# Nystrom attention and a multiplicative FFN on one core: another written order of the steps, and a later opening of the up products' buffer

## The chip, the core and the metric

The kernel runs on one core of a Trainium2 chip. The metric is the device time of one execution in microseconds (us); smaller is better. All durations are in us unless ns is written. TensorE (PE) does the matmuls, VectorE (DVE) and ScalarE (ACT) read its results out of PSUM, GpSimd (POOL) adds up landmarks and issues loads, SyncE (SP) issues loads and stores.

## The reference

Eight batches of eight heads, 576 tokens, head size 64. Attention goes through 32 landmarks per head, each the mean of 18 neighbouring rows, with a pseudo-inverse by six Newton steps; the FFN multiplies two linear maps of the result and applies two more.

```python
q_lm = q.reshape(B, H, m, S // m, D).mean(axis=3)      # m = 32; k_lm likewise
A, Bm, C = sm(q, k_lm), sm(q_lm, k_lm), sm(q_lm, k)    # softmax of scaled scores
Z = Bm.transpose(0, 1, 3, 2) / (norm_1(Bm) * norm_inf(Bm) + 1e-06)   # norms over all of Bm
for _ in range(6):
    Z = 2 * Z - Z @ Bm @ Z
x = (A @ Z @ C @ v)          # then heads joined: 4608 tokens x 512
out = (((x @ w1) * (x @ w2)) @ w3) @ w_out             # 512 -> 1024 -> 1024 -> 512
```

## The kernel before

The kernel is a set of Python generators, one per piece of work. Each `yield` ends a step. A text, `ORDER`, lists the steps of all pieces, 1,065 words: each occurrence of a word runs that piece's next step. The five engines run by themselves, each takes its own instructions in the order in which they were written, and semaphores make an instruction wait for its inputs and for its buffer. So the text alone sets the order on every engine and every queue.

A word's last number is the batch, the landmark chain (`CHAINS`: batches 0; 1, 2; 3, 4; 5, 6, 7), the weight part or the group of rows. Where a digit stands ahead of the point, it is a part of the piece.

The weights' product comes first, W = w3 @ w_out in eight row blocks:

- `K`: one warm-up matmul (L593), after seven that stand ahead of the order. `KC`: constants in six steps; the fifth is an addition and six copies on VectorE (L615, L617).
- `S.c`: w_out's row block c is split into two fp16 halves, on ScalarE, then VectorE. `T0.j`, `T1.j`: four transposes of w3's block j (L523), then a copy on ScalarE and a split on VectorE (L529); T0.0 does this in two halves. `F.j`: eight steps of three matmuls each (L537), then a copy out.
- `L`, `LO`: loads of w3 and w_out parts on SyncE. `P`, `FV`: a small copy on GpSimd, which holds the load of the next step on SyncE back. `GT.n`: a small copy on GpSimd that reads a weight part (GT.0: part 4 of w_out), so that the loads behind it in GpSimd's queue wait till the part is there. `LW.1`, `LW.0`: the up weights w2 and w1, two loads each, on GpSimd.

For each batch b:

- `LQ`, `LK`: q and k in halves, loads on GpSimd; `LV`: v on SyncE. `TQ`, `TK`: turned by VectorE (L165). `SQ`, `SK`: landmark sums (L194 to L205) in two steps, on VectorE for batch 0, else on GpSimd. `E.b`: the landmarks' exchange, for batches 0 and 1 by two matmuls and a copy, later by copies on ScalarE (L223).
- `A`, `B`, `C`: the three score matmuls (L326, L241, L269) with exponentials on ScalarE; C is then turned on VectorE. `N`, `R`: norms and squares; `I0` to `I5`: the Newton steps (L389). `V`: landmark values in three groups of matmuls (L347, L353). `M0`, `M1`: row sums of A by a matmul with ones (L366), two passes of ScalarE, one of VectorE. `Z`: Z times the values (L415).
- `G0` to `G3`: Z C v times the up weights (L438), copied out by ScalarE (G0, G2) or VectorE (G1, G3). `U0` to `U7`: the up matmuls, four for w1 (L453), a copy on ScalarE (L458), four for w2 (L453), the product on VectorE (L460) into the buffer `ab`, one for two batches, of which there are two.
- `W.n`: the down matmuls for 128 tokens in two halves of four (L495), a copy on ScalarE (L501), two stores on SyncE. W.35 is done in two column halves (L476).

PSUM has three large buffers (`big()`), used by T, E, C (two), A (two), V, M, I, G, each half of U and some W, and one each of `small()` and `acc()`. A step that opens a large one waits until the last reader of the buffer's former contents is done. The tile shapes in the profile tell two kinds of TensorE steps apart: K, F, T, E, N, M, Z, U and W use the full array (128\*128), while A, B, C, I, R (32\*32), G and V (64\*32) use tiles of it.

The pool `pab` with the buffers `ab` takes the memory of `pf`, which holds the weights' product's inputs. In the kernel before, `pf` is closed and `ab` opened when a U word first occurs:

```python
    for word in ORDER.split():
        if word not in live:
            if word[0] == "U":
                if not pab:
                    pf_scope.__exit__(None, None, None)
                    pab.append(ctx.enter_context(tc.tile_pool(name="pab", bufs=2)))
                open_ab(int(word[3:]))
```

Of the kernel before, what the change touches and what calls it, by code (L numbers as in the profile page):

```python
# [42 lines left out]
F.5 T1.6 V.0 I4.0 V.0 F.5 T0.7 LV1.3 I4.0 F.6 F.6 E.1 F.6 TQ0.2 I4.0 I5.0 E.1 F.6 F.6 I5.0 T1.7 Z.0
SK0.2 Z.0 F.6 T0.7 A.1 Z.0 A.1 T1.7 F.6 F.6 TQ1.3 LQ0.3 A.1 SK1.2 LV3.1 LW.1 LK0.4 G2.0 G0.0 F.6 F.7
T1.7 F.7 G0.0 M0.0 C.1 TQ0.3 LK1.3 SQ0.2 M1.0 G2.0 F.7 C.1 F.7 F.7 C.1 F.7 F.7 C.1 C.1 LQ0.4 G3.0
SQ1.2 G1.0 E.2 E.2 LV1.1 F.7 U0.0 G3.0 B.1 U0.0 G1.0 V.1 U0.0 U4.0 B.1 V.1 TK0.3 U4.0 B.1 V.1 U0.0
U1.0 U4.0 N.1 TK1.3 V.1 LQ1.4 U5.0 U1.0 U4.0 N.1 U5.0 U5.0 U1.0 U2.0 U5.0 U2.0 SK0.3 U1.0 R.1 U3.0
R.1 R.1 U2.0 U3.0 LQ0.5 I0.1 U3.0 LK0.5 SK1.3 U2.0 I0.1 I0.1 U7.0 U3.0 I1.1 F.7 U7.0 I1.1 TK0.4 I1.1
U6.0 W.0 LV0.2 M1.1 U6.0 U6.0 M1.1 U6.0 U7.0 I2.1 U7.0 M0.1 M1.1 M0.1 W.0 I2.1 I2.1 A.2 LV2.2 LK1.5
LK1.4 W.0 I3.1 I3.1 W.1 A.2 I3.1 I4.1 M1.1 M0.1 I4.1 A.2 W.1 I4.1 W.1 I5.1 TQ0.4 I5.1 C.2 Z.1 C.2  # L50
Z.1 I5.1 M0.1 W.2 C.2 Z.1 G0.1 TQ1.4 TK1.4 G1.1 W.2 G0.1 W.0 G1.1 U0.1 U2.1 LV1.2 C.2 U0.1 U0.1 U1.1
W.2 U1.1 SQ0.3 SQ1.3 C.2 W.3 G2.1 SQ0.4 LV3.2 U0.1 U2.1 G3.1 G2.1 V.2 V.2 V.2 U2.1 G3.1 V.2 U1.1
U2.1 SQ1.4 U1.1 U3.1 LQ1.5 U3.1 W.3 TQ0.5 U3.1 SK0.4 U4.1 E.3 SK1.4 LV1.4 U3.1 Z.2 W.3 M0.2 U4.1 Z.2
U7.1 M0.2 U7.1 M0.2 LV2.4 LK1.6 U4.1 E.3 E.4 TK0.5 U5.1 U4.1 U7.1 LV3.3 W.2 LQ0.6 U6.1 U7.1 LV2.3
U5.1 LV3.4 U6.1 Z.2 W.4 E.4 TQ1.5 M1.2 M1.2 U5.1 U6.1 TK1.5 U5.1 B.3 G2.2 M1.2 U6.1 G1.2 G2.2 G0.2
G1.2 W.4 M0.2 G0.2 A.3 M1.2 W.4 G3.2 A.3 A.3 G3.2 LQ1.6 B.3 SK0.5 W.3 W.1 W.5 U3.2 U3.2 C.3 B.3
LQ1.7 C.3 W.5 N.3 LK0.6 W.4 SK1.5 U2.2 LV0.3 LQ0.7 U0.2 C.3 U0.2 N.3 LK1.7 C.3 R.3 U3.2 W.5 U3.2
U0.2 U2.2 U0.2 W.6 SQ0.5 U2.2 U4.2 U2.2 R.3 SQ1.5 U4.2 C.3 W.6 M0.3 M0.3 U1.2 U1.2 W.6 U4.2 U6.2
TQ0.6 V.3 U4.2 U6.2 R.3 V.3 U1.2 U1.2 U6.2 U6.2 W.7 LK0.7 U5.2 I0.3 W.7 U5.2 I0.3 U7.2 I0.3 TQ1.6
I1.3 TK0.6 I1.3 U7.2 W.7 V.3 U7.2 I1.3 W.5 I2.3 W.8 V.3 I2.3 I2.3 TK1.6 W.7 U7.2 I3.3 I3.3 I3.3 W.8  # L60
M1.3 I4.3 I4.3 W.8 LV0.4 U5.2 I4.3 W.9 U5.2 M1.3 I5.3 W.8 M1.3 A.4 M0.3 A.4 W.9 W.9 I5.3 I5.3 M1.3
Z.3 SK0.6 Z.3 A.4 W.6 W.9 C.4 W.10 M0.3 C.4 Z.3 G3.3 W.10 C.4 W.10 G1.3 G3.3 C.4 G0.3 G2.3 W.11 G0.3
U2.3 G1.3 G2.3 U1.3 U2.3 C.4 U2.3 V.4 U1.3 U2.3 SK1.6 E.5 U1.3 U0.3 TQ0.7 V.4 V.4 SQ0.6 LV2.5 U0.3
LV1.5 U1.3 E.5 TQ1.7 M0.4 V.4 U3.3 M0.4 U3.3 M0.4 U3.3 W.11 U0.3 TK0.7 U3.3 U5.3 TK1.7 W.11 U4.3
SQ1.6 Z.4 U0.3 U5.3 LV1.6 U4.3 U5.3 LV0.5 U5.3 A.5 E.6 A.5 Z.4 A.5 W.12 M1.4 M1.4 LV3.6 U7.3 Z.4 E.6
U4.3 M0.4 U4.3 U7.3 M1.4 U7.3 W.12 W.11 U6.3 U7.3 M1.4 G0.4 W.12 U6.3 LV0.6 G1.4 SQ0.7 G0.4 G1.4
G2.4 W.13 SQ1.7 W.10 G2.4 C.5 C.5 SK0.7 LV3.5 U6.3 C.5 U6.3 SK1.7 U1.4 W.13 U1.4 U0.4 E.7 LV2.6 C.5
C.5 V.5 E.7 V.5 G3.4 B.5 U0.4 U0.4 W.13 W.14 B.5 U0.4 G3.4 W.14 U3.4 W.14 B.5 U2.4 V.5 U3.4 U1.4 N.5
U1.4 U2.4 W.13 W.15 W.15 N.5 U2.4 R.5 V.5 W.15 U2.4 R.5 A.6 W.16 U4.4 A.6 A.6 U4.4 M0.5 R.5 I0.5
W.14 M0.5 I0.5 I0.5 W.12 U4.4 U4.4 U5.4 I1.5 U5.4 I1.5 U3.4 I1.5 U3.4 M0.5 U5.4 U6.4 U5.4 I2.5 I2.5  # L70
U7.4 M0.5 U6.4 I2.5 U7.4 U6.4 U6.4 I3.5 W.16 I3.5 M1.5 I3.5 I4.5 W.16 M1.5 W.17 C.6 I4.5 I4.5 I5.5
M1.5 I5.5 W.17 I5.5 C.6 Z.5 M1.5 W.17 Z.5 U7.4 Z.5 W.18 W.17 I5.5 G0.5 C.6 G1.5 W.16 U7.4 G0.5 G2.5
W.18 G1.5 U0.5 U1.5 C.6 G2.5 U0.5 U1.5 U1.5 C.6 U0.5 U2.5 U1.5 V.6 V.6 U0.5 U2.5 G3.5 LV3.7 W.18
U3.5 W.19 U3.5 U3.5 G3.5 U2.5 U3.5 U2.5 W.19 U4.5 W.19 U5.5 U4.5 V.6 M0.6 U5.5 U5.5 W.18 V.6 M1.6
M0.6 LV0.7 Z.6 LV2.7 LV1.7 U5.5 M1.6 U6.5 U4.5 U6.5 W.20 Z.6 M1.6 M0.6 Z.6 G0.6 G1.6 W.19 U4.5 G2.6
W.20 G0.6 M1.6 G3.6 G1.6 G2.6 A.7 W.20 G3.6 M0.6 W.21 W.20 A.7 W.21 U7.5 A.7 U6.5 W.21 U7.5 U0.6
U7.5 U6.5 U0.6 W.22 U7.5 U0.6 W.15 U2.6 U2.6 U0.6 W.22 U1.6 C.7 W.22 W.23 U1.6 C.7 W.22 W.23 M1.7
C.7 W.23 U1.6 U3.6 W.24 W.24 C.7 M1.7 U1.6 U2.6 U5.6 U3.6 U4.6 W.24 W.25 U2.6 W.24 U5.6 W.25 C.7
M1.7 U3.6 U3.6 W.25 V.7 W.23 V.7 U4.6 V.7 W.25 V.7 U4.6 W.26 U4.6 U6.6 U6.6 Z.7 U5.6 M0.7 M1.7 W.26
Z.7 M0.7 U7.6 U6.6 U5.6 W.26 U7.6 U6.6 M0.7 W.27 W.21 Z.7 U7.6 M0.7 G0.7 G1.7 U7.6 G1.7 G0.7 W.27  # L80
U1.7 U1.7 G2.7 W.27 G2.7 G3.7 U1.7 U1.7 W.28 U4.7 U4.7 W.28 W.28 U5.7 U3.7 W.26 G3.7 U5.7 U4.7 W.29
W.28 U4.7 U3.7 U5.7 U3.7 W.29 W.29 W.29 U3.7 U5.7 U0.7 U0.7 U2.7 W.27 U0.7 U7.7 U0.7 U2.7 W.30 U6.7
U7.7 U2.7 U7.7 U2.7 W.30 U6.7 U7.7 U6.7 W.31 W.30 U6.7 W.31 W.32 W.32 W.33 W.33 W.31 W.32 W.30 W.33
W.34 W.31 W.34 W.34 W.35 W.32 W.33 W.35 W.34 W.35 W.35 W.35 W.35
"""


# [1 line left out]
def kernel(  # L89
# [358 lines left out]
    def up(st, j):  # L448
        for w in range(2):
            p = big()  # L450
            for qd in range(2):
                for c in range(2):
                    nc.tensor.matmul(p[:, c, 0:HS], st["g"][:, qd, w, 128 * j:128 * j + 128],  # L453
                                     st["ahat", qd][:, c, :], start=(qd == 0), stop=(qd == 1))
            yield
            if w == 0:
                a_sb = po.tile([128, 2, HS], FP16, name="a_sb", bufs=2)
                nc.scalar.copy(out=a_sb, in_=p[:, :, 0:HS])  # L458
# [246 lines left out]
```

## Time and profile before

| | |
|---|---|
| time, median of 3 runs | 261.96 us (261.48 to 262.25) |
| span of the profiled execution | 260.5 us |
| the profiled execution's own time | told as its span only; 1.5 us lie between it and the median |
| TensorE busy | 249.7 us (96% of the span) |
| VectorE, ScalarE, GpSimd busy | 161.5, 159.2, 119.3 us |
| first warm-up matmul, first transpose | 1.19 us, 4.16 us |
| last matmul starts | 256.1 us |

The span runs from the first to the last instruction of one profiled execution. [...]

### The profile page before, as it was taken

What the parts mean: (1) busy time and instruction counts of PE and PEld (TensorE: products, weight loads), DVE (VectorE), ACT (ScalarE), POOL (GpSimd) and SP (SyncE); (2) the same over time, 40 slices, a digit from 0 to 9 for tenths busy, and PEclk for the clock granted to TensorE, in tenths of its full rate; (3) what the DMA queues carried; (4) which work ended last, traced back from release to release, by engine and by line L of the source; (5) the groups of instructions that cost most, each with busy time, mean ns of one, the idle gap of its engine ahead of it and who ended that gap; (6) DMA issues with size and microseconds to landing.
All of it is one profiled execution on the core that took longest, in us unless ns stands there. A gap on an engine that the chain in (4) does not pass through costs nothing.

```text
span 260.5 us, 10306 instructions
## 1 busy us (share of the span) xinstructions
PE 249.7 (96%) x4480; PEld 147.9 (57%) x4480; DVE 161.5 (62%) x306; ACT 159.2 (61%) x349; POOL 119.3 (46%) x199
## 2 busy tenths in 40 slices
...
DMA packets 23357, 37.37 MB, mean 143 GB/s; under 512 B 2832, under 2 KB 11536, under 8 KB 23312
## 3 DMA queue, kind: packets, MB, share of 16 engines
...
## 4 chain that ended last, share of the span: by engine, by line
PE 82%; DVE 7%; ACT 5%; DMA 2%; issue 2%; SPq 0%; DVEq 0%; ACTq 0%
PE big L453 21%; PE acc L495 20%; PE acc L537 13%; PE big L438 5%; PE big L347 4%; PE big L389 4%; PE big L523 3%; PE small L537 2%; ACT a_sb L458 2%; DVE ab L460 2%; PE big L366 2%; PE big L495 1%; DMA wof<-in_moe_w_out_dram 1%; PE small L415 1%; PE big L326 1%
## 5 line engine op out<-in xcount | busy, mean ns | idle before, releaser
L453 PE MATMUL big<-ahat,gt 128*128 128x288 f16 x512 | 74.3, 286 | 1.3 <-ACT a_sb L458 0.7
L460 DVE TENSOR_TENSOR ab<-a_sb,big 128x576 f16<-128x576 f16 x64 | 47.1, 750 | 35.3 <-PE big L453 33.5
L495 PE MATMUL acc<-w,ab 128*128 128x512 f16 x264 | 66.7, 380 | 0.0
L453 PEld LDWEIGHTS <-gt 128*128 128x128 f16 x512 | 48.5, 98 | 22.0 <-issue 3.0
L458 ACT CAST a_sb<-big 128x576 f16<-128x576 f32 x64 | 40.2, 639 | 33.2 <-PE big L453 18.8
L194 POOL TENSOR_TENSOR tr<-qkT 128x256 f32<-128x256 f16 x56 | 37.3, 697 | 18.2 <-DVE qkT L165 16.3
L537 PE MATMUL acc<-wsp,w3t 128*128 128x512 f16 x168 | 41.6, 384 | 0.0
L495 PEld LDWEIGHTS <-ab 128*128 128x128 f16 x280 | 25.4, 98 | 27.0 <-issue 4.8
L537 PEld LDWEIGHTS <-w3t 128*128 128x128 f16 x192 | 18.4, 100 | 19.8 <-issue 3.1
L501 ACT ACTIVATE o_sb<-acc 128x512 f32<-128x512 f32 x33 | 19.8, 599 | 10.8 <-PE acc L495 9.5
L445 DVE TENSOR_SCALAR gt<-big 128x1024 f16<-128x1024 f32 x16 | 19.4, 1220 | 7.9 <-PE big L438 7.9
L165 DVE STREAM_TRANSPOSE qkT<-qkn 128x576 uint32<-128x576 uint32 x32 | 24.0, 762 | 0.0
L200 POOL TENSOR_TENSOR tr<-tr 128x256 f32<-128x256 f32 x28 | 19.8, 727 | 0.1
L443 ACT ACTIVATE gt<-big 128x1024 f16<-128x1024 f32 x16 | 15.7, 1024 | 3.4 <-PE big L438 3.3
L438 PE MATMUL big<-wup,zt 64*32 64x512 f16 x512 | 17.3, 379 | 0.3 <-ACT en L370 0.2
L347 PE MATMUL big<-vt,ent 64*32 64x64 f32 x1152 | 14.8, 225 | 0.1
L128 POOL DMA_DIRECT2D qkn<-in_k_dram x16 | 11.5, 722 | 6.9 <-DVE qkT L165 6.9
L347 PEld LDWEIGHTS big<-vt,ent 64*32 64x32 f32 x1152 | 12.7, 105 | 3.4 <-issue 2.3
L284 DVE STREAM_TRANSPOSE ent<-en 128x576 f32<-128x576 f32 x16 | 12.0, 762 | 3.3 <-ACT en L280 3.3
L375 DVE TENSOR_TENSOR ahat<-eat,en 128x576 f16<-128x576 f16 x16 | 13.8, 870 | 0.0
L280 ACT ACTIVATE en<-big 128x288 f32<-128x288 f32 x32 | 12.8, 415 | 0.5 <-PE big L269 0.5
L527 ACT ACTIVATE w3t<-big 128x512 f16<-128x512 f32 (+1 forms) x17 | 9.6, 571 | 5.6 <-PE big L523 5.3
...
## 6 DMA issues: line engine op xcount, KB each, us to landing
...
wof<-in_moe_w_out_dram SPq DMA_DIRECT2D x6, 256.0 KB, 7.4
```

The costliest lines, as they stand in the source:

```text
L165: nc.vector.transpose(out=st["qkT"][:, t, prs].rearrange("p c r q e -> p (c r q e)").bitcast(U32), in_=st["qkn"][:, t, prs, :].rearrange(" ...
L194: add(out=tr[:, c], in0=x[:, c, 0:4, :], in1=x[:, c, 4:8, :], op=ALU.add)
L200: add(out=tr[:, c, 0:2, :], in0=tr[:, c, 0:2, :], in1=tr[:, c, 2:4, :], op=ALU.add)
L347: nc.tensor.matmul(psV[32 * o:32 * o + 32, qd, 0:64], ent[sl, pr, r, :], vt[sl, pr, 64 * r:64 * r + 64], start=(r == 0), stop=(r == RT - 1 ...
L438: nc.tensor.matmul(psG[o:o + 32, qd, :], zt[rs, i, h, :], wup[rs, h, w, fs], start=(i == 0), stop=(i == 1), tile_position=(64 * qd, o))
L445: nc.vector.tensor_scalar(out=g[:, :, w, fs], in0=psG, scalar1=1.0 / ZS, scalar2=None, op0=ALU.mult)
L453: nc.tensor.matmul(p[:, c, 0:HS], st["g"][:, qd, w, 128 * j:128 * j + 128], st["ahat", qd][:, c, :], start=(qd == 0), stop=(qd == 1))
L458: nc.scalar.copy(out=a_sb, in_=p[:, :, 0:HS])
L460: nc.vector.tensor_tensor(out=st["ab"][:, j, st["t0"]:st["t0"] + S].rearrange("p (c s) -> p c s", c=2), in0=a_sb, in1=p[:, :, 0:HS], op=AL ...
L495: nc.tensor.matmul(pso[:, :], ab[:, j, t0:t0 + 128], w34[:, j, :], start=(j == 0), stop=(j == 7))
L501: nc.scalar.activation(out=o_sb, in_=pso, func=AXF.Copy, scale=1.0 / (X64 * X64))
L537: nc.tensor.matmul(psW, w3ts[j, c // 4][:, a, c % 4, :], wsp[:, b, c, :], start=(c == 0 and a + b == 0), stop=(c == 7 and a == 1))
```

## The change

The words of `ORDER` are written in another order; none is added or taken away. `open_ab` is called in `up`, just ahead of the product on VectorE, instead of ahead of a U word's first step, and closes `pf` there. The core of the diff follows; of the order, the first lines and those that hold the steps the prediction speaks of.

```diff
 ORDER = """
-T0.0 S.0 S.0 T0.0 T0.0 T0.0 T0.1 S.2 S.2 LQ0.0 T0.1 K LQ1.0 S.1 T0.1 L.2 LO.6 S.3 F.0 K F.1 S.1
-LK0.0 T0.0 KC F.0 LK1.0 T0.0 T1.0 F.0 T1.0 S.3 S.4 K T1.0 S.5 S.4 F.1 K FV.0 F.1 F.0 T1.1 T1.1 K S.6
-F.0 S.5 T1.1 KC LO.7 KC F.1 F.1 T1.2 F.1 TQ1.0 T1.2 GT.0 LK1.1 L.3 T0.2 LK0.1 S.7 F.0 S.6 F.1 TQ0.0
...
-C.0 GT.5 F.3 B.0 F.3 C.0 N.0 T0.5 KC T1.4 TQ1.1 N.0 LW.0 F.3 T1.4 T1.4 SK0.1 C.0 TQ0.1 F.4 LV2.1 F.4
-T0.5 F.4 A.0 T0.5 R.0 R.0 R.0 F.4 F.4 F.4 LQ0.2 A.0 I0.0 I0.0 T0.6 LV0.1 SK1.1 L.7 I0.0 A.0 T0.6 C.0
...
-M0.0 M1.0 C.0 TK1.2 F.5 V.0 V.0 TQ1.2 M1.0 T1.6 I3.0 F.5 F.5 TK0.2 I3.0 F.5 M1.0 I3.0 LK0.3 F.5 T0.7
...
+K GT.0 S.0 K KC K T0.0 T0.1 LQ1.0 K T0.0 T0.1 L.2 S.0 S.1 S.2 LQ0.0 T0.0 T0.1 K S.3 LO.6 F.0 T0.0
+S.1 LK1.0 S.4 T0.0 LK0.0 F.1 LO.7 LK1.1 T1.0 S.2 F.1 F.1 S.5 T1.0 F.0 LQ0.1 T1.1 T0.0 F.0 S.3 L.3
+S.5 T1.0 S.4 S.6 F.1 T0.2 T1.1 F.0 S.7 LK0.1 T0.2 LQ1.1 S.6 T1.1 F.0 T1.2 T1.2 S.7 F.0 F.0 T0.2 T1.2
+KC TQ1.0 F.0 FV.0 P.4 F.1 F.0 T0.3 T1.3 F.2 F.2 F.2 F.2 P.4 F.2 GT.2 T0.3 T1.3 F.2 F.2 L.5 F.2 T0.3
+F.1 F.2 F.1 F.1 TQ0.0 F.3 F.3 SQ0.0 TK1.0 SQ1.0 TK0.0 F.3 F.3 SK0.0 T1.3 SK1.0 F.3 TQ0.1 F.1 FV.0
+E.0 T0.4 LQ0.2 E.0 LK0.2 KC TK1.1 F.3 TK0.1 C.0 T0.4 KC B.0 C.0 F.3 B.0 T0.4 C.0 F.3 F.3 LQ1.2 B.0
+A.0 A.0 N.0 GT.3 T0.5 SK0.1 T0.5 F.4 C.0 L.6 F.4 T1.4 A.0 N.0 KC F.4 T0.5 R.0 T1.4 R.0 F.4 T1.5 R.0
+I0.0 T1.5 GT.4 T1.4 M1.0 LV0.1 M1.0 TQ0.2 F.4 I0.0 C.0 SK1.1 F.4 TQ1.1 F.4 M0.0 F.4 I0.0 M0.0 I1.0
+TK0.2 I1.0 I1.0 V.0 T1.5 LK1.2 V.0 F.4 SQ0.1 V.0 I2.0 KC F.5 T0.6 T0.6 V.0 T1.6 I2.0 SQ1.1 T0.6 F.5
+LW.1 L.7 I2.0 F.5 I3.0 T1.6 T1.6 E.1 TK1.2 F.5 I3.0 T1.7 M0.0 I3.0 I4.0 M1.0 LW.1 F.5 T1.7 E.1 F.5
+I4.0 I4.0 F.5 LW.0 I5.0 T1.7 I5.0 A.1 M1.0 LW.0 TQ1.2 F.5 Z.0 A.1 F.5 T0.7 A.1 F.6 T0.7 Z.0 C.1 GT.5
+SK0.2 F.6 Z.0 C.1 LK0.3 T0.7 SK1.2 M0.0 F.6 SQ0.2 F.6 C.1 F.6 LV2.1 LV1.1 F.6 F.6 F.6 SQ1.2 G3.0
+LK1.3 F.6 G1.0 F.7 GT.6 F.7 F.7 C.1 LV1.3 F.7 E.2 LV3.1 LQ1.3 M1.1 F.7 E.2 G1.0 LQ0.3 G3.0 F.7 F.7
+LQ1.4 C.1 M1.1 B.1 B.1 B.1 LQ0.4 G0.0 G2.0 G0.0 F.7 LK0.4 N.1 G2.0 U0.0 U1.0 U0.0 U0.0 U1.0 N.1
...
 """
...
                 nc.scalar.copy(out=a_sb, in_=p[:, :, 0:HS])
                 yield
+        open_ab(st)
         nc.vector.tensor_tensor(
             out=st["ab"][:, j, st["t0"]:st["t0"] + S].rearrange("p (c s) -> p c s", c=2),
             in0=a_sb, in1=p[:, :, 0:HS], op=ALU.mult)
...
-    pairs = {}
-
-    def open_ab(b):
+    pairs, pab = {}, []
+
+    def open_ab(st):
+        b = st["b"]
+        if not pab:
+            pf_scope.__exit__(None, None, None)
+            pab.append(ctx.enter_context(tc.tile_pool(name="pab", bufs=2)))
         if b // 2 not in pairs:
             pairs[b // 2] = pab[0].tile([128, 8, 2 * S], FP16, name="ab")
-        sts[b]["ab"] = pairs[b // 2]
-        sts[b]["t0"] = S * (b % 2)
+        st["ab"] = pairs[b // 2]
+        st["t0"] = S * (b % 2)
...
-    pab, live = [], {}
+    live = {}
     for word in ORDER.split():
         if word not in live:
-            if word[0] == "U":
-                if not pab:
-                    pf_scope.__exit__(None, None, None)
-                    pab.append(ctx.enter_context(tc.tile_pool(name="pab", bufs=2)))
-                open_ab(int(word[3:]))
             work = started(word)
```

More of the change, by code (lines that the diff above doesn't have):

```diff
@@ L32 @@
 ORDER = """
-T0.0 S.0 S.0 T0.0 T0.0 T0.0 T0.1 S.2 S.2 LQ0.0 T0.1 K LQ1.0 S.1 T0.1 L.2 LO.6 S.3 F.0 K F.1 S.1
-LK0.0 T0.0 KC F.0 LK1.0 T0.0 T1.0 F.0 T1.0 S.3 S.4 K T1.0 S.5 S.4 F.1 K FV.0 F.1 F.0 T1.1 T1.1 K S.6
-F.0 S.5 T1.1 KC LO.7 KC F.1 F.1 T1.2 F.1 TQ1.0 T1.2 GT.0 LK1.1 L.3 T0.2 LK0.1 S.7 F.0 S.6 F.1 TQ0.0
-T0.2 F.0 GT.2 S.7 T0.2 F.0 SQ0.0 T1.2 F.1 TK1.0 F.0 LQ1.1 LQ0.1 T1.3 P.4 T1.3 F.2 T1.3 F.2 SQ1.0
-T0.3 GT.3 TK0.0 F.2 P.4 T0.3 LK1.2 SK0.0 L.5 F.2 T0.3 F.2 F.2 F.2 LK0.2 F.2 F.2 T0.4 F.1 T1.5 LQ1.2
@@ L38 @@
-KC SK1.0 F.3 F.3 T0.4 T1.5 F.3 TK0.1 FV.0 F.3 GT.4 T0.4 LW.1 TK1.1 L.6 E.0 F.3 F.3 E.0 B.0 T1.5 B.0
-C.0 GT.5 F.3 B.0 F.3 C.0 N.0 T0.5 KC T1.4 TQ1.1 N.0 LW.0 F.3 T1.4 T1.4 SK0.1 C.0 TQ0.1 F.4 LV2.1 F.4
-T0.5 F.4 A.0 T0.5 R.0 R.0 R.0 F.4 F.4 F.4 LQ0.2 A.0 I0.0 I0.0 T0.6 LV0.1 SK1.1 L.7 I0.0 A.0 T0.6 C.0
-F.4 I1.0 M0.0 LQ1.3 I1.0 F.4 I1.0 I2.0 T0.6 KC SQ0.1 LW.0 F.4 T1.6 M0.0 F.5 F.5 I2.0 GT.6 I2.0 SQ1.1
-M0.0 M1.0 C.0 TK1.2 F.5 V.0 V.0 TQ1.2 M1.0 T1.6 I3.0 F.5 F.5 TK0.2 I3.0 F.5 M1.0 I3.0 LK0.3 F.5 T0.7
@@ L43 @@
[L43 to L84, printed above, removed]
+K GT.0 S.0 K KC K T0.0 T0.1 LQ1.0 K T0.0 T0.1 L.2 S.0 S.1 S.2 LQ0.0 T0.0 T0.1 K S.3 LO.6 F.0 T0.0
+S.1 LK1.0 S.4 T0.0 LK0.0 F.1 LO.7 LK1.1 T1.0 S.2 F.1 F.1 S.5 T1.0 F.0 LQ0.1 T1.1 T0.0 F.0 S.3 L.3
@@ new lines @@
+LK1.3 F.6 G1.0 F.7 GT.6 F.7 F.7 C.1 LV1.3 F.7 E.2 LV3.1 LQ1.3 M1.1 F.7 E.2 G1.0 LQ0.3 G3.0 F.7 F.7
+LQ1.4 C.1 M1.1 B.1 B.1 B.1 LQ0.4 G0.0 G2.0 G0.0 F.7 LK0.4 N.1 G2.0 U0.0 U1.0 U0.0 U0.0 U1.0 N.1
+TK0.3 R.1 U0.0 U4.0 TK1.3 U1.0 V.1 V.1 U4.0 F.7 R.1 R.1 LK1.4 U1.0 V.1 I0.1 V.1 I0.1 SK0.3 U5.0
+LV1.2 TQ1.3 U4.0 I0.1 I1.1 U5.0 U4.0 I1.1 U5.0 I1.1 U2.0 U5.0 U2.0 TQ0.3 I2.1 U2.0 SK1.3 U7.0 I2.1
+LV2.3 I2.1 U3.0 U2.0 LV0.2 I3.1 I3.1 U7.0 U3.0 U7.0 I3.1 U7.0 M0.1 U3.0 M0.1 I4.1 U6.0 U3.0 I4.1
+SQ0.3 I4.1 U6.0 TQ1.4 U6.0 M1.1 W.0 LV3.2 M0.1 LV2.2 A.2 U6.0 A.2 A.2 I5.1 TK0.4 W.0 I5.1 Z.1 W.0
@@ new lines @@
+Z.1 M0.1 M1.1 C.2 SQ1.3 I5.1 LK0.5 C.2 Z.1 W.1 G0.1 C.2 E.3 G1.1 LQ0.5 G2.1 TQ0.4 W.1 C.2 LQ1.5 G0.1
+G1.1 LK1.5 U1.1 U0.1 G2.1 U1.1 SQ0.4 U1.1 G3.1 C.2 U0.1 V.2 U1.1 V.2 G3.1 LV0.3 V.2 W.1 U2.1 U0.1
+TK1.4 V.2 U2.1 W.2 U2.1 U0.1 U2.1 M1.2 U3.1 Z.2 W.1 M0.2 M1.2 SQ1.4 U3.1 Z.2 U6.1 TQ0.5 U3.1 M0.2
+U3.1 U6.1 W.2 M1.2 SK0.4 TK1.5 W.2 U6.1 Z.2 U6.1 U7.1 U7.1 TK0.5 TQ1.5 U4.1 SK1.4 U4.1 W.3 SQ0.5 W.2
+U7.1 U7.1 LK0.6 U4.1 E.3 E.4 LV1.4 E.4 U5.1 W.3 U5.1 U4.1 W.3 U5.1 M1.2 B.3 B.3 A.3 W.4 U5.1 A.3
@@ new lines @@
+G3.2 B.3 A.3 G0.2 M0.2 G3.2 N.3 N.3 W.4 G0.2 C.3 SQ1.5 C.3 R.3 M0.2 R.3 LK1.6 SK0.5 LV3.4 W.4 G2.2
+G1.2 C.3 G1.2 W.5 G2.2 U0.2 W.5 R.3 U0.2 I0.3 M0.3 LQ0.6 C.3 W.0 U0.2 I0.3 I0.3 U1.2 W.5 U0.2 W.6
+M0.3 W.3 U3.2 C.3 U1.2 TK0.6 I1.3 M0.3 LV3.3 W.5 I1.3 U3.2 U1.2 LQ1.6 U3.2 W.4 LK1.7 I1.3 TK1.6 U7.2
+W.6 U1.2 U3.2 I2.3 U7.2 U2.2 M0.3 W.6 SK1.5 I2.3 U7.2 I2.3 U4.2 U2.2 U2.2 W.7 U7.2 U4.2 U2.2 M1.3
+M1.3 U4.2 U6.2 W.7 M1.3 U6.2 U5.2 I3.3 E.5 U4.2 I3.3 V.3 W.7 V.3 V.3 LV2.4 W.6 I3.3 U5.2 TQ1.6 V.3
@@ new lines @@
+I4.3 U6.2 I4.3 W.8 I4.3 I5.3 U6.2 M1.3 LK0.7 I5.3 A.4 W.8 LQ0.7 Z.3 I5.3 A.4 SK0.6 C.4 LQ1.7 A.4
+U5.2 TQ0.6 W.8 LV0.4 SK1.6 Z.3 C.4 LV3.5 W.9 Z.3 U5.2 C.4 E.5 G3.3 SQ0.6 C.4 G3.3 G0.3 W.9 G2.3 C.4
+G0.3 G1.3 TQ0.7 V.4 SQ1.6 V.4 W.9 G2.3 G1.3 V.4 U1.3 V.4 U1.3 U7.3 U7.3 U7.3 W.10 TQ1.7 U1.3 U3.3
+E.6 U7.3 LV2.5 U1.3 U0.3 U3.3 U0.3 Z.4 SQ0.7 Z.4 M1.4 M1.4 U3.3 W.10 SQ1.7 E.6 TK1.7 W.8 TK0.7 LV0.5
+SK0.7 W.10 A.5 U3.3 Z.4 U5.3 W.7 A.5 W.11 U0.3 A.5 U5.3 M0.4 M1.4 W.10 W.11 SK1.7 U6.3 M0.4 U0.3
+U2.3 U5.3 W.11 W.9 U2.3 U5.3 W.12 G1.4 U6.3 G1.4 G0.4 M0.4 U2.3 U2.3 LV1.5 G0.4 W.12 M1.4 U4.3 U6.3
```

18 lines of the change are left out of this document (added).

## The prediction

> **What bounds the kernel now.** I read the busy time and the chain first.
>
> ```profile
> PE 249.7 (96%) x4480; PEld 147.9 (57%) x4480; DVE 161.5 (62%) x306; ACT 159.2 (61%) x349; POOL 119.3 (46%) x199
> ...
> PE 82%; DVE 7%; ACT 5%; DMA 2%; issue 2%; SPq 0%; DVEq 0%; ACTq 0%
> ```
>
> TensorE has 82% of the chain that ended last. A new order removes no instruction, so it can gain in two ways only: fewer gaps on TensorE, or steps that cost less because of what stands next to them. For the second I read TensorE's timeline; columns are start, length, instruction, and the start-to-start distances are what counts.
>
> ```profile
> 126.55 1.03 PE L495 MATMUL acc<-w,ab 128*128 128x512 f16 x4
> 127.41 0.65 PE L453 MATMUL big<-ahat,gt 128*128 128x288 f16 x4
> 127.99 0.45 PE L389 MATMUL big<-sz__2461,tz__2389 32*32 32x64 f32 x32
> ...
> 139.01 1.04 PE L495 MATMUL acc<-w,ab 128*128 128x512 f16 x4
> 139.98 0.63 PE L438 MATMUL big<-wup,zt 64*32 64x512 f16 x16
> 140.54 1.04 PE L495 MATMUL acc<-w,ab 128*128 128x512 f16 x4
> 141.50 1.49 PE L438 MATMUL big<-wup,zt 64*32 64x512 f16 x48
> 142.93 1.04 PE L495 MATMUL acc<-w,ab 128*128 128x512 f16 x4
> ```
>
> The down half-step L495 that a full-array step follows lasts 127.41 - 126.55 = 0.86; the one that a tiled step (64\*32) follows lasts 139.98 - 139.01 = 0.97. The up half-step L453 in front of a tiled one lasts 0.58, elsewhere 0.49. So passing from full array to tiles costs some 0.093 (the median difference). Passing back costs too: one project step L438 between two down steps takes 0.56, three in a row 1.43, which is 0.44 + 0.44 + 0.55.
>
> I cut all matmul records at the steps of the order and took each kind's median start-to-start time, once with a full-array step next and once with a tiled one: down half 0.863/0.957, up half 0.490/0.583, product third 0.647/0.741, project 0.548/0.435, values first group 0.657/0.481, second 0.628/0.470, scores C 0.455/0.371. With these the old order sums to 239.6. Before its first step lie 4.2, and after its last 4.2, so of the span of 260.5 there are 12.5 left: true gaps. 3.4 of them lie before 10.6, and 9.1 later. The largest of those:
>
> ```profile
> PE big L326 <- DVE w3t L529: 1.2, 1, 1.2
> ...
> PE big L523 <- issue: 0.9, 1, 0.9
> PE big L453 <- ACT a_sb L458: 0.7, 1, 0.7
> ```
>
> The first is A.0 at 37.7 and the second the transposes T0.7 at 52.0; the third stands at 107.2. All later ones are below 0.6. The start:
>
> ```profile
> 1.19 3.17 PE L593 MATMUL big<-warm 128*128 128x512 f16 x7 [1.19 <-DVE warm L589]
> 4.16 0.66 PE L523 MATMUL big<-ident,w3f 128*128 128x128 f32 x2
> 5.97 1.54 PE L523 MATMUL big<-ident,w3f 128*128 128x128 f32 x6 [1.15 <-DVE w3t L529]
> ...
> 7.73 1.49 PE L537 MATMUL acc<-wsp,w3t 128*128 128x512 f16 x3
> ...
> 10.63 0.81 PE L537 MATMUL acc<-wsp,w3t 128*128 128x512 f16 x3
> ```
>
> Three product matmuls take 1.28 start to start at 7.73 and 0.65 at 10.63: TensorE runs at half speed until 10.5, where the trace's record of the granted clock begins with full speed.
>
> **The change, part by part.** *Counts.* Both orders hold the same 1,065 words, each equally often, five warm-up K among them. Busy time of the other engines stays.
>
> *The buffer's opening.* In the new order the last reader of the old memory (F.7's last matmuls; W.8 and W.17 for later pairs) stands ahead of the first up matmul anyway, so the product on VectorE waits for nothing new: 0. The cover is at least the up step's own two matmul groups and copy (0.49 + 0.49 + 0.64).
>
> *Neighbours.* Going through both orders, 60 of the 419 passages between TensorE steps lead from full array to tiles before, 49 after: 11 x 0.093 = -1.02. On the way back: no values step is cut open by a full-array step any more (first groups 2 to 0, second 1 to 0): 2 x 0.176 + 0.158 = -0.51; one project step fewer in front of a full step, -0.11; two scores C fewer, -0.17; the rest +0.07. Sum **-1.74** (237.9 against 239.6). TensorE does this work whatever else waits, so this counts in full where TensorE is the bound, and not where another engine ends last; bounds 0 and -1.74; I take all, since gaps are 12.5 of 260.5.
>
> *Gaps in the middle.* Beside each step of each order I wrote the TensorE time ahead of it, and added up in the written order what VectorE, ScalarE and GpSimd have to do for it, by the rows' durations (up copy 0.64, up product 0.75, turn 0.77, split 0.68, landmark sums 2.6 and 3.75), PSUM and copy buffers included. Where such a sum is in arrears, TensorE waits. For the old order the deepest arrears of separate stretches are 1.8 (to 38 of TensorE time), 0.4, 1.3, 3.1 (93 to 116), 1.9 and five of 0.3 to 0.5: 10.3, where the trace has 9.1 less 1.1 for T0.7, which is no engine's doing: 8.0. So the ledger overstates by a factor of 0.78. For the new order: 2.3, 4.5 (58 to 119), 0.7, 1.2, 0.3: 9.0, times 0.78 is 7.0. That is **-1.0**. Where they sit: first, KC's copies
>
> ```profile
> 35.48 2.29 DVE L617 COPY bt<-eye 128x32 f32<-128x32 f32 x6
> ```
>
> which made A.0 wait, now stand, with the addition in their step, in front of T0.5's split, R.0 and T1.4's split, whose buffer M1.0 takes: 2.5 + 0.7 + 0.7 + 0.7 = 4.6 of VectorE against 2.6 of TensorE work up to M1.0, so M1.0 waits some 2 in place of A.0's 1.2. Then GpSimd: from TQ1.1 it has batch 1's SQ, four LW, batch 2's SK and SQ with loads between, 22 in a row, and with VectorE's 22 ahead of it E.2's copies come 2.4 late for B.1; E.2 stands in ScalarE's queue, so M1.1, B.1, G0.0 and the first up copies queue behind it, and ScalarE, with 21 of work in 23, only catches up after 85. In return 93 to 118 and 140 to 155 get lighter. Bounds: the old 8.0 again (0), and half of the new ledger (-3.5).
>
> *T0.7's 1.1* names no releaser; the load of its w3 rows was issued at 36.2, behind two loads of up weights (30 to 50). The new order asks for those weights after SQ1.1, behind it. It can stay (0) or go (-1.1): **-0.5**.
>
> *The start.* K moves: three stand ahead of T0.0 now, so T0.0 starts at 1.19 + 10 x 0.427 = 5.5 instead of 4.2, but T0.0, T0.1 and two more K then run without the 1.15 gap for a copy. At 10.5 the old order had 3.0 of priced work behind it. If half speed lasts till then again, the new one has (10.5 - 4.2) / 2 = 3.2: -0.2. The old start reached full speed after 4.6 of unbroken work (5.97 to 10.5); the new one is unbroken from 1.2, which would be 5.8, and (5.8 - 4.2) / 2 + 4.7 = 5.5: -2.5, if weights are there. GT.0, now first on GpSimd, holds the first q and k loads until w_out's part 4 lands (10.7 before, sooner without q between), which speeds w3 and w_out. But T0.3 now comes at 12.5 of priced work, 12.5 + 7.6 = 20.1 on the old start's clock; its rows landed at 20.7 and can hardly be there before 18.5 to 19.5, which leaves 0.6 to 1.6 of a gain. I take **-0.8**, nearer to the slow end.
>
> [...]
>
> Sum: -1.74 - 1.0 - 0.5 - 0.8 = -4.0. The profiled execution's span is 260.5; the median 261.96 is 1.5 above, which I leave as it is: **258.0**.
>
> **Rivals.** *Neighbours alone:* ScalarE's queue behind E.2 costs what the old waits cost, start and T0.7 give nothing: -1.7, 260.2. For: 21 of 23 is dense, and one late copy feeds the next. Against: the old order had the like at 93 to 116 (3.1). 0.15.
>
> *The clock opens by 5.8* and the weights are there: the start gives 2.1 (the 2.5 less what T0.3's rows cut off) in place of 0.8, and T0.7's wait goes entirely: 258.0 - 1.3 - 0.5 = 256.2. For: ten K without a break. Against: arrivals. 0.15. [...]
>
> *Nothing gained:* the switches' 1.7 lie where another engine ends last, and new waits take the rest: 261.2 to 262.7. 0.10.
>
> *Slower: the first k loads come late.* Held by GT.0, they are issued near 10.5 to 11.5 instead of 4.7 and 5.4, behind them come w3's. E.0 needs them turned and summed: TK1.0, SQ1.0, TK0.0, SK0.0, T1.3, SK1.0 are 0.8 + 2.1 + 0.8 + 1.2 + 0.7 + 2.1 = 7.6 of VectorE, and E.0 is due near 23.8 + 6.8 = 30.6, so k must land by 22.9. Landed before: 17.2 and 20.5 after 12.5 and 15.1 in flight; the same flights give 23.5 and 26, a wait of 1. Every us beyond is paid in full, since all later stages hang on E.0 and VectorE's queue stands; past a wait of 4, a landing near 27, the change loses. With flights of 17 to 19, as the longest here, 28 to 30: waits of 5 to 7, 263 to 265. For: loads queue up to 19 in this stretch. Against: the same bytes are ahead, only in another sequence. 0.15.
>
> **How the numbers follow.** Forecast 0.45, the rivals as above. Faster by over 0.3% (0.8, what a measurement of this kernel can tell): 0.45 + 0.15 + 0.15 = 0.75; within 0.10; slower 0.15. The lower end is the clock rival, 256.0; the upper reaches through "nothing gained", 262.4.
>
> **What would show it.** Down half-steps of 0.97 become rarer, and project and values steps stand in runs. Gaps near the copies L617 end at a landmark or ones matmul (L366) instead of A.0; ScalarE waits on GpSimd's landmark sums before L223 for batch 2. The step is right on the start if three product matmuls take 0.65 before 9. I am wrong if E.0 waits several us because q and k land late, or if TensorE's gaps after 10.6 exceed 9.

## The result and the profile after

The changed kernel is slower: 275.20 us (median of 4, 271.79 to 277.18) against 261.78 (261.48 to 262.25), a ratio of 1.047 with a 95% interval of 1.040 to 1.053. Its profiled execution is the shortest, 271.79 with a span of 270.0. The other three show a mean granted clock of 0.972 to 0.975 in place of 0.986, and the median stands 3.4 above it. The two traces differ by 270.0 - 260.5 = 9.5, so some 4 of the 13.4 us between the medians lie outside what the traces show. A ratio takes in only those executions that lie within 1.5% of the kernel's shortest, of which e3 below has one alone and so no ratio.

The page of the changed kernel, busy time, TensorE's row and its clock in 40 slices, the instruction queue's transfers, and the chain:

```profile
PE 250.6 (93%) x4480; PEld 150.6 (56%) x4480; DVE 161.0 (60%) x306; ACT 158.5 (59%) x349; POOL 117.0 (43%) x199
...
PE   8999994999978999999999999997999996999993
...
PEclk9999999599999999999999999999999999999999
...
q8 instruction: 35, 0.57, 0.9%
...
PE 77%; DVE 9%; ACT 6%; issue 5%; DMA 1%; SPq 0%; DVEq 0%; ACTq 0%
```

The instructions are as many as before, and TensorE is busy for as long. It stands still near 45 us, smaller dents follow near 80, 184 and 227, and the chain has 5% of "issue", time in which the engine waited for nothing that the profile shows. In one slice the clock is half. TensorE's waits (the line that waits, the releaser, total, times, longest):

```profile
PE big L347 <- issue: 5.0, 3, 2.4
PE big L353 <- issue: 3.9, 1, 3.9
PE big L453 <- DVE ab L461: 1.5, 1, 1.5
...
PE acc L496 <- issue: 1.0, 2, 0.7
```

Before, the longest wait was 1.2. L347 and L353 are the values step V. The largest wait in TensorE's timeline:

```profile
43.56 0.27 PE L353 MATMUL big<-sums,eye 64*32 64x1 f32 x10
47.77 0.27 PE L353 MATMUL big<-sums,eye 64*32 64x1 f32 x3 [3.94 <-issue]
```

The same stretch in busy time per window (length, then PE, weight loads, VectorE, ScalarE, GpSimd, then clock, DMA share, GB/s), first the changed kernel, then the kernel before:

```profile
41.70:43.70 2.00, 2.00 (x174) 1.84 (x173) 1.37 (x4) 1.00 (x3) 1.92 (x4) 1.00 1.09 197
43.70:47.70 4.00, 0.13 (x17) 0.04 (x5) 0.00 (x0) 0.00 (x0) 3.84 (x8) 0.93 1.03 216
47.70:54.00 6.30, 6.23 (x36) 3.31 (x36) 2.72 (x6) 1.92 (x4) 2.30 (x5) 0.50 1.08 197
```

```profile
41.70:43.70 2.00, 2.00 (x27) 1.06 (x25) 0.79 (x2) 0.53 (x2) 2.00 (x4) 1.00 1.11 232
43.70:47.70 4.00, 4.00 (x52) 2.13 (x51) 3.40 (x9) 2.92 (x7) 3.77 (x8) 1.00 1.18 201
```

Two things are seen. In the 4 us in which TensorE stands, VectorE and ScalarE do nothing at all, and GpSimd adds up landmarks and issues loads of the up weights: nobody is making an operand for V.0 or I2.0. And in the 2 us ahead TensorE has 174 matmul records and 173 weight loads, where the kernel before has 27 and 25 at that time, in another step. From 47.2 on, still in the stop, the clock is half for 6.8 us.

**Where the gaps stand.** I numbered TensorE's records from 0 (weight load and matmul, each pass of a four-byte matmul by itself, as V shows with 160 matmul records for 80 written and with 80 on two-byte operands in e4, and the 50 semaphore and drain instructions) in order of time. The page shows 35 transfers of instructions with 0.57 MB, 16,384 bytes each; TensorE has 9,010 records, 35 times 256 and a rest. A gap here runs from the start of one record to the start of the next; the page takes it from the end of the last matmul, and its waits are 0.2 to 0.4 shorter. Eight gaps over 0.3, the six that the page calls "issue" among them, lie right ahead of a record whose number is 193 more than a multiple of 256. (The 1.5 put down to VectorE's product is one of them too.) In each of the seven below, one transfer of that queue ends 1.2 to 1.5 before work resumes: the next block's. It starts only about when the block ahead of it is entered, 0.2 before to 1.5 us after in six of the seven, 2.9 after in the first, where the DMA share is 1.03 to 1.10 (0.00 to 0.66 over the other six blocks and gaps), and it takes 0.9 to 1.5. So a block that TensorE runs through too fast leaves it without instructions: block and gap together last 2.2 to 3.9 us, 5.4 in the first. Worked out from the changed kernel's records:

| time, step | block lasted | gap |
|---|---|---|
| 43.7, V.0 | 1.27 | 4.11 |
| 79.6, V.1 | 1.27 | 2.59 |
| 138.4, W.8 (after I) | 2.10 | 1.04 |
| 181.0, V.5 | 1.57 | 0.65 |
| 183.6, U5.4 (after I) | 1.96 | 1.77 |
| 202.0, W.19 (after V.6) | 2.67 | 0.71 |
| 226.2, V.7 | 1.35 | 2.42 |

With one of 0.32 at 101.7, in V.2, their sum is 13.6. The kernel before has a single such gap over 0.3, 1.33 at 52.0: T0.7's, at record 961, also 193 more than a multiple of 256. Its blocks are not all longer: three of 2.8 to 3.3 us, at 186.7, 77.0 and 149.4, pass without a stop, and no block lies wholly inside a values step.

The start, TensorE's timeline: the clock's record opens at 6.2 instead of 10.5, three product matmuls take 0.65 from 6.90 on.

```profile
1.19 4.45 PE L598 MATMUL big<-warm 128*128 128x512 f16 x10 [1.19 <-DVE warm L594]
5.43 1.20 PE L524 MATMUL big<-ident,w3f 128*128 128x128 f32 x6
6.47 0.59 PE L598 MATMUL big<-warm 128*128 128x512 f16 x2
6.90 0.81 PE L538 MATMUL acc<-wsp,w3t 128*128 128x512 f16 x3
```

### The profile page after: what moved, and what is told of

Read it like the earlier page. It is cut to its first block, busy times and chain, and to the rows that moved or that the text cites. A ratio compares the mean times of both kernels' runs of the same rounds, so it can differ in the third digit from the quotient of the medians.

```text
span 270.0 us, 10326 instructions
## 1 busy us (share of the span) xinstructions
PE 250.6 (93%) x4480; PEld 150.6 (56%) x4480; DVE 161.0 (60%) x306; ACT 158.5 (59%) x349; POOL 117.0 (43%) x199
## 4 chain that ended last, share of the span: by engine, by line
PE 77%; DVE 9%; ACT 6%; issue 5%; DMA 1%; SPq 0%; DVEq 0%; ACTq 0%
PE big L453 22%; PE acc L496 19%; PE acc L538 9%; PE big L347 5%; PE big L438 4%; PE big L389 4%; PE big L524 2%; PE big L598 2%; DVE qkT L165 2%; PE big L366 2%; ACT small L249 1%; PE small L415 1%; PE small L538 1%; ACT en L280 1%; PE big L269 1%
## 5 line engine op out<-in xcount | busy, mean ns | idle before, releaser
L496 PE MATMUL acc<-w,ab 128*128 128x512 f16 x264 | 67.4, 380 | 1.6 <-issue 1.0
L538 PE MATMUL acc<-wsp,w3t 128*128 128x512 f16 x168 | 42.2, 393 | 0.0
L496 PEld LDWEIGHTS <-ab 128*128 128x128 f16 x280 | 26.2, 98 | 26.7 <-issue 5.2
L347 PE MATMUL big<-vt,ent 64*32 64x64 f32 x1152 | 15.0, 225 | 5.1 <-issue 5.0
L347 PEld LDWEIGHTS big<-vt,ent 64*32 64x32 f32 x1152 | 13.5, 105 | 7.1 <-issue 6.2
L443 ACT ACTIVATE gt<-big 128x1024 f16<-128x1024 f32 x16 | 16.1, 1025 | 1.5 <-PE big L438 1.5
L530 DVE SCALAR_TENSOR_TENSOR w3t<-big,w3t 128x512 f16<-128x512 f32 (+1 forms) x17 | 11.1, 655 | 5.9 <-ACT w3t L528 5.7
L370 ACT ACTIVATE en<-big 128x576 f32<-128x576 f32 x16 | 10.3, 652 | 7.2 <-PE big L366 6.0
L128 POOL DMA_DIRECT2D qkn<-in_q_dram x16 | 11.8, 737 | 4.1 <-issue 4.1
```

The source lines that it names most:

```text
L347: nc.tensor.matmul(psV[32 * o:32 * o + 32, qd, 0:64], ent[sl, pr, r, :], vt[sl, pr, 64 * r:64 * r + 64], start=(r == 0), stop=(r == RT - 1 ...
L496: nc.tensor.matmul(pso[:, :], ab[:, j, t0:t0 + 128], w34[:, j, :], start=(j == 0), stop=(j == 7))
L538: nc.tensor.matmul(psW, w3ts[j, c // 4][:, a, c % 4, :], wsp[:, b, c, :], start=(c == 0 and a + b == 0), stop=(c == 7 and a == 1))
```

## Experiments

The theory is **instruction supply**, as above. Its rivals: **data** (V and its successors wait for operands by a path that the profile names badly) and **clock** (the half-speed stretch is the whole loss). The part on the buffer can be no cause: with the old order it compiles to the same instructions, in the same order and with the same waits, on all five engines, and e7, which has it, is faster than the kernel before.

Border gaps below are those over 0.3 at block borders; half speed is the time at half clock between the clock's opening and the last matmul. The ratio is to runs of the kernel before taken along with each experiment. The 0.3 of e7 and e11 is no stop: it is the passage into a project step, which takes 0.31 in the kernel before too, at 62.5 us for one, 84 records behind a border.

| | border gaps: number, sum, longest | half speed | time | ratio to before, 95% |
|---|---|---|---|---|
| before | 1, 1.3, 1.3 | 0 | 261.8 | |
| after | 8, 13.6, 4.1 | 6.8 | 275.2 | 1.047 (1.040 to 1.053) |
| e2_before_shift | 6, 6.6, 1.9 | 0 | 270.3 | 1.028 (1.023 to 1.034) |
| e3_after_shift | 8, 18.2, 3.1 | 20.5 | 281.4 | |
| e4_after_bf16 | 3, 4.7, 2.2 | 6.8 | 258.5 | 0.987 (0.982 to 0.991) |
| e5_v_moved | 8, 7.6, 1.5 | 0 | 266.3 | 1.021 (1.015 to 1.027) |
| e6_graft | 0 | 6.8 | 264.4 | 1.009 (1.006 to 1.012) |
| e7_start_moved | 1, 0.3, 0.3 | 0 | 259.8 | 0.991 (0.988 to 0.995) |
| e8_spread | 3, 3.1, 1.4 | 0 | 266.5 | 1.018 (1.014 to 1.022) |
| e9_spread_tail | 3, 3.5, 2.1 | 3.4 | 264.4 | 1.009 (1.006 to 1.011) |
| e10_start_shift | 8, 9.4, 2.0 | 3.4 | 269.2 | 1.028 (1.025 to 1.031) |
| e11_weight_earlier | 1, 0.3, 0.3 | 0 | 259.9 | 0.993 (0.991 to 0.995) |

### The borders moved, the order kept: e2 and e3

```diff
+HALVED = (0, 1, 2)
...
-                nc.tensor.matmul(psW, w3ts[j, c // 4][:, a, c % 4, :], wsp[:, b, c, :],
+                w = DM // 2 if j in HALVED else DM
+                for x in range(0, DM, w):
+                    nc.tensor.matmul(psW[:, x:x + w], w3ts[j, c // 4][:, a, c % 4, :], wsp[:, b, c, x:x + w],
```

> The kernel before in its own order, but the 72 matmuls of the first three products F.0 to F.2 are each cut into two of 256 columns: the same work, the same waits, 144 more records (a weight load and a matmul each) ahead of everything from about 35 us. Theory 'instruction supply' (TensorE's instructions come in blocks of 256, a block is fetched only when the one ahead of it is entered, and a block that lasts under about 3.6 us runs dry, 5.4 where the DMA queues are crowded): the block borders move by 144 records and now cut the short stretches, so new gaps at about 74 (0.9), 99 (2.2), 132 (1.7), 166 (1.9) and 225 us (2.3), the gap of 1.3 at 52 shrinks below 0.5; sum of gaps at borders 1.3 -> about 9, time 261.8 -> 267 to 270. Theory 'data' (the gaps of the new order are waits for operands that the profile names badly): order and waits are those of before, so 261.3 to 262.6 and the gap at 52 stays 1.3. Theory 'clock' (the half-speed stretch is the whole loss): nothing opens at 35 to 50 us, 261.3 to 262.6.

Measured: 270.28 (267.9 to 272.1), 8 us more for the same work in the same order. The profiled execution is the shortest; its span is 5.6 longer than that of before, and its border gaps are 5.3 more. TensorE's timeline at T0.7 in the kernel before, then the same steps in e2:

```profile
49.65 2.76 PE L537 MATMUL acc<-wsp,w3t 128*128 128x512 f16 x12
53.37 0.66 PE L523 MATMUL big<-ident,w3f 128*128 128x128 f32 x4 [0.95 <-issue]
```

```profile
49.62 2.76 PE L540 MATMUL acc<-wsp,w3t 128*128 128x512 f16 x12
52.22 0.60 PE L524 MATMUL big<-ident,w3f 128*128 128x128 f32 x4
...
53.85 0.27 PE L348 MATMUL big<-vt,ent 64*32 64x64 f32 x4
55.08 0.27 PE L354 MATMUL big<-sums,eye 64*32 64x1 f32 x15 [0.96 <-issue]
```

T0.7 no longer waits, and the gap has gone to the border's new place, in V.0's last group. That I had not placed: there I expected 0.4. Four of the five others came where they were computed, 1.41 at 99.4, 0.73 at 133.7, 1.02 at 168.3 and 1.85 at 228.9, each smaller than forecast (6.6 in sum against 9). The fifth, at 74, did not: a block of 2.7 us passed there without a stop, so the 3.6 of my theory is no sharp limit. One of 0.45 at 117.3 I had not computed. Data and clock are ruled out for this kernel: no wait was changed, and the clock stayed full in the profiled execution.

> The changed kernel in its own order with the same cut: 144 more records ahead of everything from about 33 us. Instruction supply: the gap of 4.1 us at 43.7 shrinks below 1 and the granted clock stays full there; those at 79.6, 181, 183.6 and 226 vanish or move, and new ones stand at about 83 (2.3), 102 (2.0), 137 (2.1), 140 (1.0), 148 (2.0), 182 (2.3), 200 us (2.0): their sum stays 13 to 15, the 2.75 us of the half-speed stretch are gone: 268 to 271 (profile of the changed kernel: 271.8; median 275.2). Data: gaps at 43.7, 79.6 and 226.2 stay where they are: 271.5 to 276. Clock: as data, since nothing in the order of waits changes.

Measured: 281.44 (275.5 to 284.0; 282.1 in the profiled execution), a miss in time. The gaps did move (42.9, 78.5, 102.4, 121.0, 139.5, 154.3, 191.3, 211.0), six of them inside V; the one at 226 is gone, 154 had none before and 102 only 0.3. But the one at 43 only shrank to 2.96, the sum rose to 18.2, and the clock fell five times, as the profile's row shows:

```profile
PEclk9999996899988999999979799999899999999999
```

What I had not seen is that the clock can fall after gaps of 2 to 3 us too: none of this run's is over 3.1.

### Fewer instructions, the same waits: e4

```diff
+    def upper(x):
+        return x.bitcast(mybir.dt.bfloat16)[:, 1::2]
...
-                nc.tensor.matmul(psV[32 * o:32 * o + 32, qd, 0:64], ent[sl, pr, r, :],
-                                 vt[sl, pr, 64 * r:64 * r + 64], start=(r == 0), stop=(r == RT - 1),
+                nc.tensor.matmul(psV[32 * o:32 * o + 32, qd, 0:64], upper(ent[sl, pr, r, :]),
+                                 upper(vt[sl, pr, 64 * r:64 * r + 64]), start=(r == 0), stop=(r == RT - 1),
```

> The changed kernel with the values step V reading only the upper two bytes of its four-byte operands (bfloat16; the lower half of the mantissas is left out): one pass in place of two, 160 records a step in place of 320, same order, same producers and waits. V itself gets 0 to 1 us shorter, eight times: 0 to -8. Instruction supply: gaps at block borders fall from 13.3 to 1.5 to 3.5 (what is left at about 82, 141 and 183), the one at 43.7 is gone and with it the half-speed stretch (2.75): 250 to 260. Data: V and I2.0 wait as before, only V's own passes are saved, the gap before I2.0 stays over 3 us and the clock drops after it: 264 to 275. Clock: as data unless the gap goes.

Measured: 258.53, inside the supply theory's range and 5 below the lowest figure of data. The edit also shortens V's own passes and, with fewer records, moves every border behind V.0; the trace tells these apart. The gap of 4.1 is gone (V.0 runs 42.97 to 43.73, I2.0 follows at once), the border gaps fall from 13.6 to 4.7, which is 8.9 of the 12.1 us by which the span shrinks. Two of those left, 2.2 and 1.65, each had 3.4 at half speed behind it.

### The values steps alone moved: e5

V.1 to V.7 are moved likewise.

```diff
-I1.0 TK0.2 I1.0 I1.0 V.0 T1.5 LK1.2 V.0 F.4 SQ0.1 V.0 I2.0 KC F.5 T0.6 T0.6 V.0 T1.6
+V.0 V.0 I1.0 TK0.2 I1.0 I1.0 T1.5 LK1.2 F.4 SQ0.1 I2.0 KC F.5 T0.6 V.0 V.0 T0.6 T1.6
...
```

> The changed kernel's order with the 32 words of the values steps V.0 to V.7 alone moved, by 14 places earlier to 6 later, so that longer steps stand between their parts; every other step stands as in the changed kernel. Instruction supply: the gaps at block borders go from 13.3 to 4.8 to 7 (left: about 1.4 to 1.8 at V.0, 1.2 to 1.5 at W.8, 2 around I0.5 and U5.4 of heads' chain 5, 0.5 to 0.8 at W.19), no gap is long enough for a half-speed stretch (2.75), and TensorE waits 2 to 3.5 us more for data where V no longer covers the Newton steps: span 270.0 -> 260 to 264, time 262 to 266. Data: the waits go where V goes, 270 to 275. Clock alone: 271.8 - 2.75 = 269.

Measured: 266.32, 0.3 above the range, with border gaps of 7.6 where 4.8 to 7 were expected, and well under the 270 of data. No border gap is over 1.5, the clock stays full, and 9 of the 13.4 us are won back with 32 words, none of which changes what V reads.

### The start on the old order: e6 and e7

```diff
 e6: words 1 to 64 of the changed order | ... T1.2 T1.2 S.7 F.0 | FV.0 KC KC F.1 ... left of before
 e7: words 1 to 168                     | ... C.0 SK1.1 F.4 | LK1.2 LW.1 T1.5 ...    left of before
```

> The first 64 words of the changed order (up to about 12 us), the rest in the order of before. If the start's part of the prediction is right, the granted clock opens at about 6.2 us in place of 10.5, nothing behind is touched, the gap of 1.3 at T0.7 (52 us) stays: 261.9 - 2.2 = 259 to 260. If the start of before hides its half-speed time behind w3's loads, or the 64 words cost it back in front of E.0: 261 to 262.5.

Measured: 264.36, outside both ranges. The clock opened at 5.8, but TensorE then waited 5.5 for w3's rows,

```profile
PE big L524 <- DMA w3f<-in_moe_w_dram: 5.5, 2, 3.2
```

and lost the clock for another 6.8. The gate P.4 holds those loads until the first k rows are there, which the changed order asks for later; the old order's next words need them sooner. So I took my joint, not the start, to be at fault:

> The first 168 words of the changed order (up to about 40 us), what is left of the order of before behind them, so that the first loads of w3, q and k keep the neighbours that they have in the changed kernel. Instruction supply: behind 40 us the stretches are those of before, gap at a border of 0.8 to 1.2 near 49 us, sum 1.7 to 3; the start gives its 2.2 to 2.8 us (clock open at about 6), the joint costs 0.5: 259 to 261.5. If the whole order of the changed kernel is at fault, its beginning too: 264 and over. If the first 64 words lost in the other joint by the loads alone, no wait of TensorE for w3 over 1 us is left here.

Measured: 259.83, 2 us under before and 15 under the changed kernel, with no stop at a border (1.7 to 3 in sum were expected) and no wait for w3. The old order's stop at T0.7 is gone too, since its border has moved. This version beats both kernels at full arithmetic.

### Every block made long enough: e8 and e9

```diff
 e8, words 175 to 193
-I1.0 TK0.2 I1.0 I1.0 V.0 T1.5 LK1.2 V.0 F.4 SQ0.1 V.0 I2.0 KC F.5 T0.6 T0.6 V.0 T1.6 I2.0
+M0.0 T1.5 I1.0 F.4 M0.0 I1.0 F.5 T0.6 TK0.2 LK1.2 I1.0 F.5 SQ0.1 KC SQ1.1 I2.0 M0.0 T0.6 V.0
 e9, the last 60 words as in the changed kernel; the end, e8 and e9
-... W.34 W.35 W.33 W.33 W.35 W.31 W.35 W.35 W.35
+... W.35 W.31 W.34 W.33 W.35 W.35 W.35 W.35 W.35
```

> The changed order from word 120 on with steps moved by a few places (500 of 1,065 by more than 3, 121 by more than 10) so that every block of 256 instructions lasts over 3.8 us by the durations of the changed kernel's trace, 5.6 where the transfers crowd, with the same steps and the same start. Instruction supply: gaps at borders 13.3 -> under 2, no half-speed stretch, TensorE's waits for data 10.8 -> 8.5, neighbours 1.1 dearer: span 252 to 255, time 254 to 257. Data: the waits stay or move: 262 to 275. Clock alone: 269.

Measured: 266.47, 9.5 more than the range's top. The border gaps fell to 3.1 (under 2 was expected), no stretch at half speed is left, and the matmuls ended at 256.2 instead of 265.8. But the span ends 7.9 later, not 4.1,

```profile
PE   8999998899999999999999999999999999999980
```

because I had let outputs slip behind each other on SP; and the waits for data, which I had worked out to fall to 8.5, were 9.0 by the trace where the changed kernel has 6.8. By itself e8 does not part the theories: its time lies in the range that I gave for data.

> The order of e8_spread up to word 1,005; its last 60 words stand as in the changed kernel. In e8_spread TensorE's last matmul ended at 256.2 and the span 7.9 us later, since the last outputs went out late in one row on SP; with the changed kernel's end that is 3.6 to 4.2 us again and nothing else moves: span 264.1 - 4 = 260, time 261.5 to 263. If instead the matmuls of the end come later by as much, 265 to 267.

Measured: 264.37, between the two ranges. The end is 4.1 again. Of the 3.8 gained there 2.2 went, since the last matmul ends at 258.4: V.0's border gap was 2.1 this time, where e8 had 1.4, since its block's fetch started 4.9 after the border instead of 3.8, and the clock fell for 3.4 after it.

### The borders moved under the best order: e10, and a load: e11

e10 is e7 with e2's edit.

> The order of e7_start_moved (259.8, gaps at borders 0.3) with the matmuls of F.0 to F.2 cut in two: 144 more records ahead of about 35 us, nothing else. Instruction supply: gaps near 71 (0.9 to 1.2), 99 (2.1 to 2.4), 134 (1.3 to 1.6), 170 (1.8 to 2.1) and 233 us (2.2 to 2.5): sum about 8.5 to 10, in e2_before_shift 6.6 came where 9.7 was computed, so 6 to 9 here: 266 to 269, and what the start gave is there all the same, 2 us under e2_before_shift (270.3). Data: 259 to 260.5.

Measured: 269.24, 0.2 above the range, with gaps at 97.5, 132.1, 166.6 and 229.7 among others, in sum 9.4. The gap computed for 71 did not come. The time is only 1.0 under e2, not 2; the border gaps are 2.8 more than there, and 3.4 us ran at half speed.

```diff
 e11: e7 with one word moved
-... I3.0 F.5 M1.0 I3.0 LK0.3 F.5 T0.7 F.5 ...
+... I3.0 F.5 M1.0 I3.0 LW.1 LK0.3 F.5 T0.7 F.5 ...
```

> e7_start_moved with one word moved: the second LW.1, the last of the four loads of up weights, 39 words earlier, ahead of LK0.3. In e7_start_moved it is issued at 56.4 and lands at 66.7, and G1.0 waits 1.6 for it near 65, the longest wait on TensorE there. Issued near 48.5 it lands by 61: the wait goes, 258.0 to 258.7. If the q and k loads of batch 3, 0.65 later on GpSimd's queue, or another late step take its place: 259 to 260.5. Instruction supply: the same words in the same order on TensorE, so no new gap at a border.

Measured: 259.94, no different from e7. The wait for the weights is gone, and near 68 us B.1 now waits 0.8 for batch 2's exchange, T waits 0.5 for one w3 load.

## Why the prediction was wrong, by its steps

Ahead of the first step, behind the last and at the price table's durations, both spans close: 260.5 = 8.4 + 239.6 + 12.5 and 270.0 = 8.4 + 237.9 + 23.7. The prices made on the old trace hold in the new one: from 150 to 170 and from 230 on, where no border gap stands, they leave 0.1 us in all. The 23.7 of gaps split into 0.6 in the start, 13.6 at block borders, 2.75 of lengthening in the half-speed stretch (48.4 to 53.9) and 6.8 of the rest; the 12.5 before into 3.4, 1.3, 0 and 7.8.

| term | forecast | measured |
|---|---|---|
| neighbours | -1.74 | -1.7, by the price table |
| buffer | 0 | 0, the same program with the old order |
| gaps in the middle | -1.0 | -1.0 |
| T0.7 | -0.5 | a block border, counted there |
| start | -0.8 | -2.8 |
| block borders | not in the sum | +12.3 |
| half speed after the longest gap | not in the sum | +2.75 |
| sum | -4.0 | +9.5 |

- *What bounds the kernel*: the failing step is the sentence that a new order "removes no instruction, so it can gain in two ways only". It can also lose in a third: when its instructions come. "Counts" was costed at nothing because the number stays; how many fall into how short a time was never counted. The runs showed stops at the borders of instruction blocks in its place, 12.3 more, and 2.75 of half speed behind the longest.
- *Neighbours*: right in size, and it is where the loss was made. I booked 0.51 for values steps that no full-array step cuts open any more. By the traces six of the eight values steps stand in two pieces before and one after; my three were only those that a full-array step cuts. Uncut, V runs 256 records in 1.3 us. The four stops inside V.0, V.1, V.5 and V.7 are 9.8 of the 13.6; e5 cut just these four open again and won 9. What I counted as a gain is what empties the block. Where the borders fall counts as well: e2 leaves V as it was and has 5.3 more of stops.
- *Middle*: the sum was right, its places were not. M1.0 waits 0.2 where I had 2.
- *T0.7*: wrong. I put a gap that "names no releaser" down to a load. e2 moved it with the border, at unchanged loads. It was the one visible case of what was to come.
- *Start*: mis-sized, -2.8 against -0.8. The clock opened early and w3's rows were in time, as the clock rival had it. But that the unbroken K opened the clock is not shown. e2 starts with the words of before, with the same break at 4.8 to 6.0, and its clock opens at 4.48; six transposes that lasted 1.54 in the kernel before last 0.88:

```profile
5.96 0.88 PE L524 MATMUL big<-ident,w3f 128*128 128x128 f32 x6 [1.25 <-DVE w3t L530]
22.10 0.66 PE L524 MATMUL big<-ident,w3f 128*128 128x128 f32 x4 [0.30 <-DMA w3f<-in_moe_w_dram]
```

  The early clock gained nothing in e2: 0.9 ahead of before at 9.7, it is level at 22.1, where it waits for w3's rows (22.09 before). So it may be the order of the first steps and loads that gains, and the 10.5 on which I rested belongs to one execution. e7 has 2.1 of time from this start, with the stop of 1.3 at T0.7 gone and a wait of 1.6 for weights added.
- *The slower rival*: its sign came, its mechanism did not. The first q and k landed at 16.1 to 20.4, not 23.5 to 26, and E.0 waits for none of them.
- *What would prove me wrong*: gaps over 9 after 10.6; they are 23, the lengthening at half speed included. The rule caught the failure, not its cause.

What stays open: why the other executions of the changed kernel have a lower mean clock. Worked out from 0.986 and 0.975 they spend some 6 us more at half speed, which would fit more gaps near 2 us with half speed behind them, as in e4, but their traces were not kept and this is not shown. Open too is when a fetch begins: why it starts up to 3.2 us ahead of a border and up to 4.4 behind in the changed kernel's trace.
